# Two-chunk weight halves, a merged FFN step, and one unit's transpose on TensorE, in a kernel of block-wise linear attention followed by a bilinear FFN

## The chip, the cores and the metric

One core of one Trainium2 chip runs the whole kernel. The metric is the device time of one execution in microseconds (us), the median of the runs shown. The profile is of one execution; its span runs from the first to the last instruction.

## What is computed

The input is q, k and v (batch 4, 8 heads, 768 positions, head size 64), a decay `lam` for each head, and three weight matrices. The attention is linear with decay, computed in blocks, with a running state:

```python
intra = (q_blk @ k_blk.T * decay_mask) @ v_blk      # each batch and head
inter = (q_blk * lam_pow) @ kv_state
out_blk = intra + inter
kv_state = lam_block * kv_state + (k_blk * rev_pow).T @ v_blk
```

Its output is laid out as x, 3072 tokens by 512, and the FFN follows:

```python
a = x @ w_a          # 512 -> 1536
b = x @ w_b          # 512 -> 1536
out = (a * b) @ w_out   # 1536 -> 512
```

## The kernel before

**Units and groups.** The work is cut into 24 *units*, each one block of 128 positions of one batch element with all eight heads (six units to a batch element). Units are gathered into eight *groups* of 4, 1, 2, 4, 4, 4, 4 and 1 units (`GROUPS`). The FFN of a group runs on TensorE (PE) while the attention of later units is woven in between. The first four units are done in a packed form ahead of everything; the change does not touch them.

**One unit's attention** is made of pieces, named by letters in a hand-written plan:

- P (or PK and PV apart): the scaling of k and q to a tile `qk` in bf16, mostly on POOL (L262, L267), and the cast of v to `vb` (L276), on DVE for unit 7 and later. Then `pump()` issues further loads.
- T: `qk` transposed on PE as eight 128x128 transposes into a PSUM bank (L299), which ACT copies to `qkT` (L301). Units listed in `DMA_T` have no T: P issues a DMA transpose from SP's queue instead (L285).
- S: the scores of the unit (L313, two PSUM banks) and two masks on DVE (L330).
- V: the unit's k and v products added to a bank `kvd` (L369), and the state copied from it by DVE to `st` (L401). The next V writes the same bank.
- O, O2 and Q: the output of one unit, of two, or of two units together with the scores of the next two: products with the state (`inter`, L345), with the masked scores (L355), and the copy to the FFN's input `xT` on ACT (L362).

**The FFN of a group** has 12 *parts*, one for each 128 columns of w_a and w_b. A part is four matmuls for a and four for b (L439), a copy `a_sb` of a on ACT (L447), and a product `ab` on DVE (L452). Then come the matmuls with w_out (L472). After every part, and at points between the w_out matmuls, `hook(slot)` runs what `PLAN` lists for that group and slot: slots 0 to 11 are the parts, 12 and later lie in the w_out stage. Engines run in program order, so the plan fixes the order on every engine.

**The weights** are loaded in f32 through twelve staging buffers `wst` in the order of `pending`, and cast to bf16 by `cast_w`. w_a and w_b come in six chunks of 256 columns, which a DMA reads in rows of 1,024 bytes; w_out comes in six chunks of two row blocks, in rows of 2,048 bytes. Group 0's FFN follows the arrival: it takes the chunks in steps (`W_STEPS`), all a parts of a step before its b parts, and casts the next step's chunks meanwhile, a on DVE and b on ACT.

**Loads of q, k and v** are issued by SP in the order of `pending`. `pump()` lets them through up to a distance from the unit last prepared: `LOOKAHEAD` is 3 units at first and 2 once more than 8 units are in use, with 2 at nine units and 1 at ten. These loads, the DMA transposes and nearly all stores share SP's queue, which works in order. PSUM banks are taken in a ring of seven.

Of the kernel before, what the change touches and what calls it, by code (L numbers as in the profile page):

```python
# [22 lines left out]
def _bc(ap, dims):  # L23
# [3 lines left out]

GROUPS = (4, 1, 2, 4, 4, 4, 4, 1)
W_CHUNKS = (256,) * 6
W_STEPS = ((0, 1), (2,), (3,), (4,), (5,))  # L30
W_BUFS = 12
LOOKAHEAD = {9: 2, 10: 1}
DMA_T = (7,) + tuple(range(9, 24))
KEEP_GROUPS = 3
PACK = 4

# [8 lines left out]
        (35, "PK", 5), (35, "PV", 5)],  # L45
    1: [(0, "V", 4), (2, "T", 5), (3, "PK", 6), (6, "PV", 6), (6, "S", 5), (7, "T", 6),
        (10, "S", 6), (12, "O2", (5, 6)), (13, "P", 7)],
    2: [(0, "V", 6), (1, "P", 8), (4, "T", 8), (4, "P", 9), (8, "S", 7),
        (8, "S", 8), (9, "V", 7), (6, "P", 10), (10, "V", 8),
        (12, "Q", (7, 8, 9, 10)), (12, "P", 11), (13, "V", 9), (14, "P", 12),  # L50
        (14, "O2", (9, 10))],
    3: [(3, "S", 11), (3, "S", 12)],
# [13 lines left out]
def kernel(  # L66
# [11 lines left out]
    nc = tc.nc  # L78
    B, H, S, D = q.shape
# [46 lines left out]
    def load_x(w, u):  # L126
        b, nb = divmod(u, NB)
        t = ld_pool.tile([128, H, D], F32, name=w + "f", tag=w + "f")
        nc.sync.dma_start(out=t, in_={"q": qr, "k": kr, "v": vr}[w][b, nb])
        raw[u, w] = t  # L130

    wa_sb = singles.tile([128, KS, d_ff], BF16, name="wa_sb")
    wb_sb = singles.tile([128, KS, d_ff], BF16, name="wb_sb")
# [4 lines left out]
    staged = {}  # L138
    w_off = [sum(W_CHUNKS[:i]) for i in range(len(W_CHUNKS) + 1)]

    def load_w(kind, c):
        t = wst_pool.tile([128, 1024], F32, name="wst", tag="wst")
        if kind == "o":
            t = t[:].rearrange("p (k n) -> p k n", k=2)
            nc.sync.dma_start(out=t, in_=wo_r[:, 2 * c:2 * c + 2, :])
        else:
            w = W_CHUNKS[c]
            t = t[:, :KS * w].rearrange("p (k n) -> p k n", k=KS)
            r = wa_r if kind == "a" else wb_r
            nc.sync.dma_start(out=t, in_=r[:, :, w_off[c]:w_off[c + 1]])  # L150
        staged[kind, c] = t

    def cast_w(kind, c, eng):
        t = staged.pop((kind, c))
        if kind == "o":
            dst = wo_sb[:, 2 * c:2 * c + 2, :]
        else:
            dst = (wa_sb if kind == "a" else wb_sb)[:, :, w_off[c]:w_off[c + 1]]
        if eng == "act":
            nc.scalar.copy(dst, t)  # L160
        elif eng == "pool":
            nc.gpsimd.tensor_copy(dst[:, :, :128], t[:, :, :128])  # L162
            nc.gpsimd.tensor_copy(dst[:, :, 128:], t[:, :, 128:])
        else:
            nc.vector.tensor_copy(dst, t)
        pump()

    pending = []
    for cs in W_STEPS:
        pending += [("a", c) for c in cs] + [("b", c) for c in cs]  # L170
# [5 lines left out]
    used = {"u": 0}  # L176

    def pump():
        while pending:
            kind, c = pending[0]  # L180
            if kind in "abo":
                if len(staged) >= W_BUFS:
                    return
            elif c >= used["u"] + LOOKAHEAD.get(used["u"], 2 if used["u"] > 8 else 3):
                return
            pending.pop(0)
            if kind in "abo":
                load_w(kind, c)
            else:
                load_x(kind, c)  # L190
# [15 lines left out]
    for w, src in (("q", q), ("k", k)):  # L206
        x4_r = src[0, :, 0:PACK * BLK, :].rearrange("h (p r) d -> p h (r d)", r=PACK)
        n_h = 4 if w == "q" else 2
        for h in range(0, H, n_h):
            t = wst_pool.tile([128, 1024], F32, name=w + "4", tag="wst")[:, :n_h * 256]  # L210
            nc.sync.dma_start(out=t.rearrange("p (h x) -> p h x", h=n_h), in_=x4_r[:, h:h + n_h])
            t = t.rearrange("p (h r d) -> p h r d", h=n_h, r=PACK)
# [3 lines left out]
    for u in range(n0):  # L216
        load_x("v", u)
    pump()


# [39 lines left out]
    def make_ks(u, eng):  # L260
        qk = prep_pool.tile([128, 2, H, D], BF16, name="qk", tag="qk")
        eng_of(eng).tensor_mul(qk[:, 1], raw.pop((u, "k")),  # L262
                               lp_k[:, u % NB].to_broadcast([128, H, D]))
        U[u] = dict(qk=qk, kn=qk[:, 1])

    def make_qs(u, eng):
        eng_of(eng).tensor_mul(U[u]["qk"][:, 0], raw.pop((u, "q")),  # L267
                               lp_q[:, u % NB].to_broadcast([128, H, D]))
# [10 lines left out]
    def prep_k(u):  # L279
        make_ks(u, "dve" if u < n0 + 2 else "pool")  # L280
        make_qs(u, "pool")
        used["u"] = u + 1
        if u in DMA_T:
            qkT = qkT_pool.tile([128, 2, HP, 128], BF16, name="qkT", tag="qkT")
            nc.sync.dma_start_transpose(  # L285
                out=qkT[:].rearrange("p j hp i -> p (j hp) i"),
                in_=U[u]["qk"][:].rearrange("p j h d -> p (j h d)"))
            U[u]["qT"], U[u]["kT"] = qkT[:, 0], qkT[:, 1]
# [155 lines left out]
    def a_part(f, xT, gt, cuts=None):  # L444
        ps = half(wa_sb, f, xT, gt, "a_ps", cuts)
        a_sb = a_pool.tile([128, 512], BF16, name="a_sb", tag="a")
        nc.scalar.copy(a_sb[:, :gt], ps[:, :gt])  # L447
        return a_sb

    def b_part(f, xT, gt, a_sb, ab):  # L450
        ps = half(wb_sb, f, xT, gt, "b_ps")
        nc.vector.tensor_mul(ab[:, f, :gt], a_sb[:, :gt], ps[:, :gt])  # L452
# [22 lines left out]
    def ffn(u0, n, xT, hook, first, last):  # L475
        gt = n * BLK
        ab = ab_pool.tile([128, FC, 512], BF16, name="ab", tag="ab")
        if first:
            for i, cs in enumerate(W_STEPS):
                nxt = W_STEPS[i + 1][0] if i + 1 < len(W_STEPS) else None  # L480
                fs = range(w_off[cs[0]] // 128, w_off[cs[-1] + 1] // 128)
                a_sbs = [a_part(f, xT, gt, ((0, gt - BLK), (gt - BLK, gt)) if f == 0 else None)
                         for f in fs]
                if i == 0:
                    cast_w("b", cs[1], "act")
                elif nxt:
                    cast_w("a", nxt, "dve")
                for n_f, (f, a_sb) in enumerate(zip(fs, a_sbs)):
                    b_part(f, xT, gt, a_sb, ab)
                    hook(f)  # L490
                    if i == 0 and n_f == 1:
                        cast_w("a", nxt, "dve")
                if nxt:
                    cast_w("b", nxt, "act")
            ops = [ps_bank("op", [128, d_model], F32, hold=True) for _ in range(n)]
            slot = FC
            for c in range(FC // 2):
                for t in range(n):
                    out_mms(ops[t], ab, t, range(2 * c, 2 * c + 2))
                    if c == FC // 2 - 1:  # L500
                        store(u0 + t, ops[t], 0, d_model)
                    hook(slot)
                    slot += 1
            bank["held"].clear()
            return
        for f in range(FC):
            a_sb = a_part(f, xT, gt)
            b_part(f, xT, gt, a_sb, ab)
            hook(f)
        for t in range(n):  # L510
            op = ps_bank("op", [128, d_model], F32, ffn=True)
            if last and t == n - 1:
                for lo, hi in ((0, 256), (256, 384), (384, 512)):
                    if lo:
                        op = ps_bank("op", [128, d_model], F32, ffn=True)
                    out_mms(op, ab, t, range(FC), lo, hi)
                    store(u0 + t, op, lo, hi, nc.scalar if hi == d_model else None)
                return
            out_mms(op, ab, t, range(FC // 2))
            hook(FC + 2 * t)  # L520
            out_mms(op, ab, t, range(FC // 2, FC))
            store(u0 + t, op, 0, d_model)
            hook(FC + 2 * t + 1)
# [135 lines left out]
    for g, n in enumerate(GROUPS):  # L659
# [6 lines left out]
        def hook(slot, plan=plan):  # L666
            for name, us in plan.get(slot, ()):
                if name == "C":
                    cast_w("o", us, "dve")
                elif name == "PK":  # L670
                    prep_k(us)
                elif name == "PV":
                    prep_v(us)
                elif name == "P":
                    prep_k(us)
                    prep_v(us)
                elif name == "W":
                    store_kept()
                elif name == "T":
                    piece_T(us)  # L680
                elif name == "S":
                    piece_S(us)
                elif name == "V":
                    piece_V(us)
                elif name == "O":
                    pieces_O((us,))
                elif name == "O2":
                    pieces_O(us)
                else:
                    pieces_O(us[:2], us[2:])  # L690
# [31 lines left out]
```

## Time and profile before

| | |
|---|---|
| median of 3 runs | 235.05 us (234.89 to 235.6) |
| the profiled execution | 235.05 us, span 233.3 us |
| granted clock of PE | 1.000 |
| PE busy | 225.2 us, 97% |
| DVE, ACT, POOL busy | 117.6, 89.8, 50.7 us |
| DMA transposes | 16, median 4.3 us from issue to landing |
| loads of w_a and w_b | 12 of 512 KB, 8.6 us to landing |
| loads of q, k, v after the packed units | 64 of 256 KB, 4.6 to 5.1 us to landing |

Busy time is what an engine spent in instructions. In the timelines quoted later a line has the start in us, the time in us of a run of like instructions, engine, line of the kernel, operation, output<-inputs, their shape and how many; brackets at the end give how long the engine had stood before it and which instruction released it. In a list of waits a line says who waited for whom, the total in us, how often, and the longest.

Group 0's FFN begins at 18.4 us. Its a and b parts take until 39.6 us. Group 1's FFN lies between 51.3 and 62.2 us, group 2's between 62.2 and 85.0 us.

### The profile page before, as it was taken

To read this page: it belongs to the slowest core of one execution; us is meant where nothing else is said; L and a number is where in the kernel's file an instruction comes from. 1 tells how busy PE (TensorE), PEld (TensorE's weight loads), DVE (VectorE), ACT (ScalarE), POOL (GpSimd) and SP (SyncE) were. 2 spreads that over 40 slices of the span, in tenths; PEclk is the share of its full clock that TensorE was granted. 3 is DMA by queue.
4 is the path that set the end of the run, shared out by engine and by line. 5 is a ranking of instruction groups with operands and counts; after the bars stand their busy time and mean duration, and the time that the engine had idled before them with its cause. 6 is when DMAs were issued, how large, how long until landed. Compare 5 with 4: busy or idle time off the path is not lost.

```text
span 233.3 us, 4513 instructions
## 1 busy us (share of the span) xinstructions
PE 225.2 (97%) x1771; PEld 124.4 (53%) x1771; DVE 117.6 (50%) x204; ACT 89.8 (38%) x171; POOL 50.7 (22%) x65
## 2 busy tenths in 40 slices
PE   7898999999997999999999999999999999999994
PEld 2584444459696654454544454544454544444493
DVE  0894857536469645775235674235573224332050
ACT  3586553066451333342243342333332333332261
POOL 6052000237451552433300643001200000000000
PEclk9999999999999999999999999999999999999999
DMA  4999999999896999999959997229300220000311
GB/s 154 301 276 351 348 366 299 294 219 209 183 209 137 218 165 217 224 149 229 340 203 213 229 176 122 90 85 208 71 3 0 90 93 0 1 0 9 128 45 48
DMA packets 97477, 39.10 MB, mean 168 GB/s; under 512 B 84400, under 2 KB 92976, under 8 KB 97456
## 3 DMA queue, kind: packets, MB, share of 16 engines
q1 hardware_dynamic: 97168, 38.74, 73.9%
q8 instruction: 14, 0.23, 0.4%
q10 hardware_dynamic: 288, 0.07, 0.1%
q14 instruction: 7, 0.06, 0.1%
HBM read 28.32 MB, written 6.29 MB: 148 GB/s over the span
## 4 chain that ended last, share of the span: by engine, by line
PE 90%; DVE 3%; DMA 3%; ACT 2%; issue 1%; SPq 0%; DVEq 0%
PE a_ps L439 27%; PE b_ps L439 26%; PE op L472 26%; PE o_ps L355 3%; DMA q<-in_q_dram 3%; PE kq L313 2%; PE o_ps L345 2%; DVE m L330 2%; PE kvd L369 1%; ACT scratch L565 1%; PE tps L299 1%; DVE scratch L542 1%; DVE st L401 1%; PE kq L590 1%; PE kv L369 0%
## 5 line engine op out<-in xcount | busy, mean ns | idle before, releaser
L452 DVE TENSOR_TENSOR ab<-a_sb,b_ps 128x512 bf16<-128x512 bf16 (+2 forms) x96 | 52.2, 551 | 78.9 <-PE b_ps L439 58.1
L439 PE MATMUL a_ps<-xT,wa_sb 128*128 128x512 bf16 (+3 forms) x388 | 77.0, 324 | 0.7 <-ACT scratch L575 0.7
L439 PE MATMUL b_ps<-xT,wb_sb 128*128 128x512 bf16 (+2 forms) x384 | 77.1, 326 | 0.0
L447 ACT CAST a_sb<-a_ps 128x512 bf16<-128x512 f32 (+2 forms) x96 | 45.5, 480 | 66.2 <-PE a_ps L439 65.8
L472 PE MATMUL op<-wo_sb,ab 128*128 128x512 bf16 (+2 forms) x312 | 65.6, 363 | 0.0
L439 PEld LDWEIGHTS <-wb_sb 128*128 128x128 bf16 x384 | 34.5, 98 | 28.6 <-ACT wb_sb L160 0.2
L439 PEld LDWEIGHTS <-wa_sb 128*128 128x128 bf16 x388 | 33.9, 98 | 29.0 <-POOL wa_sb L162 0.8
L472 PEld LDWEIGHTS <-ab 128*128 128x128 bf16 x312 | 28.8, 98 | 29.9
L330 DVE TENSOR_TENSOR m<-kq,lotri 128x512 bf16<-128x512 f32 x47 | 29.3, 681 | 19.0 <-PE kq L313 18.5
L262 POOL TENSOR_TENSOR qk<-kf,lp_k 128x512 bf16<-128x512 f32 x18 | 18.8, 1042 | 75.9 <-DMA kf<-in_k_dram 66.0
L267 POOL TENSOR_TENSOR qk<-qf,lp_q 128x512 bf16<-128x512 f32 x20 | 22.1, 1105 | 22.5 <-DMA qf<-in_q_dram 22.5
L467 ACT COPY o_sb<-op 128x512 f32<-128x512 f32 (+2 forms) x19 | 10.3, 540 | 34.0 <-PE op L472 34.0
L362 ACT CAST xT<-o_ps 128x512 bf16<-128x512 f32 x22 | 12.0, 588 | 18.6 <-PE o_ps L355 18.1
L401 DVE TENSOR_TENSOR st<-kvd,bdiag 128x512 bf16<-128x512 f32 x18 | 12.3, 682 | 3.7 <-PE kvd L369 2.9
L276 DVE CAST vb<-vf 128x512 bf16<-128x512 f32 x17 | 11.1, 655 | 0.1
L198 PE MATMUL idle<-idle_sb 128*128 128x128 bf16 (+1 forms) x31 | 7.3, 376 | 1.3 <-DVE idle_sb L193 1.3
L355 PE MATMUL o_ps<-m,vb 128*64 128x128 bf16 x192 | 7.8, 222 | 0.0
L301 ACT COPY qkT<-tps 128x1024 bf16<-128x1024 bf16 x4 | 4.0, 1012 | 9.4 <-PE tps L299 9.4
L276 POOL CAST vb<-vf 128x512 bf16<-128x512 f32 x7 | 4.7, 674 | 13.4 <-DMA vf<-in_v_dram 13.4
L345 PEld LDWEIGHTS <-st 128*128 128x128 bf16 x80 | 5.4, 98 | 3.3 <-DVE st L401 0.6
L313 PE MATMUL kq<-qkT 64*128 64x128 bf16 x160 | 6.6, 218 | 0.0
L355 PEld LDWEIGHTS <-vb 128*64 128x64 bf16 x192 | 5.7, 109 | 1.4
(57 smaller groups left out, 86.1 us busy)
## 6 DMA issues: line engine op xcount, KB each, us to landing
vf<-in_v_dram SPq DMA_DIRECT2D x24, 256.0 KB, 5.1
qf<-in_q_dram SPq DMA_DIRECT2D x20, 256.0 KB, 4.6
kf<-in_k_dram SPq DMA_DIRECT2D x20, 256.0 KB, 4.6
out_dram<-o_sb SPq DMA_DIRECT2D x16, 256.0 KB, 2.0
wst<-in_moe_w_a_dram SPq DMA_DIRECT2D x6, 512.0 KB, 8.6
wst<-in_moe_w_b_dram SPq DMA_DIRECT2D x6, 512.0 KB, 8.7
wst<-in_moe_w_out_dram SPq DMA_DIRECT2D x6, 512.0 KB, 8.6
out_dram<-o_kept SPq DMA_DIRECT2D x7, 256.0 KB, 2.8
```

The lines of the kernel that those rows point to most:

```text
L262: eng_of(eng).tensor_mul(qk[:, 1], raw.pop((u, "k")), lp_k[:, u % NB].to_broadcast([128, H, D]))
L267: eng_of(eng).tensor_mul(U[u]["qk"][:, 0], raw.pop((u, "q")), lp_q[:, u % NB].to_broadcast([128, H, D]))
L276: eng_of(eng).tensor_copy(vb, vf)
L313: nc.tensor.matmul(kq[i][:, hp, :], lhsT=d["kT"][p, hp, :], rhs=d["qT"][p, hp, :], start=True, stop=True, skip_group_check=True)
L330: nc.vector.tensor_mul(m, kq[i], lotri_bc)
L355: nc.tensor.matmul(d["o"][p, hp, :], lhsT=d["vb"][:, 2 * hp + i, :], rhs=d["m"](i, hp), start=(first and hp == 0), stop=True, skip_group_c ...
L362: nc.scalar.copy(xT[:, :, col:col + BLK], o_ps)
L401: nc.vector.tensor_mul(st[:].rearrange("p hp i d -> p hp (i d)"), ps[:].rearrange("p hp i d -> p hp (i d)"), bdiag_bc)
L439: nc.tensor.matmul(ps[:, lo:hi], lhsT=w_sb[:, s, f * 128:(f + 1) * 128], rhs=xT[:, s, lo:hi], start=(s == 0), stop=(s == KS - 1), skip_gro ...
L447: nc.scalar.copy(a_sb[:, :gt], ps[:, :gt])
L452: nc.vector.tensor_mul(ab[:, f, :gt], a_sb[:, :gt], ps[:, :gt])
L472: nc.tensor.matmul(op[:, lo:hi], lhsT=ab[:, f, t * 128:(t + 1) * 128], rhs=wo_sb[:, f, lo:hi], start=(f == 0), stop=(f == FC - 1))
```

## The change

- Unit 7's `qk` is transposed on PE (a T at slot 1 of group 2) and no longer by DMA. Units 9 to 23 are transposed by DMA as before.
- In group 2 the scores of units 7 and 8 move from slot 8 to slot 6, and V of unit 7 from slot 9 to slot 7. V of unit 8 stays at slot 10. P of unit 10 stays at slot 6, but its vb cast now follows the masks on DVE.
- `LOOKAHEAD` is 3 units up to nine units in use and 2 above.
- The last two chunks of w_a and of w_b (columns 1024 to 1535) are loaded as two halves of the contraction, in rows of 512 columns (2,048 bytes), and cast as such. Both halves are needed for any of these columns.
- Group 0's FFN handles these columns in one step of four parts. The loads come in the order a, a, b, b where it was a, b, a, b, and the step before casts both a halves on DVE and both b halves on ACT.
- The store of the last 128 columns of the output goes out from ACT's queue in both kernels.

```diff
 W_CHUNKS = (256,) * 6
-W_STEPS = ((0, 1), (2,), (3,), (4,), (5,))
+W_STEPS = ((0, 1), (2,), (3,), (4, 5))
+W_HALVES = (4, 5)
 W_BUFS = 12
-LOOKAHEAD = {9: 2, 10: 1}
-DMA_T = (7,) + tuple(range(9, 24))
+LOOKAHEAD = (3, 2)
+DMA_T_FROM = 9
...
-    2: [(0, "V", 6), (1, "P", 8), (4, "T", 8), (4, "P", 9), (8, "S", 7),
-        (8, "S", 8), (9, "V", 7), (6, "P", 10), (10, "V", 8),
+    2: [(0, "V", 6), (1, "T", 7), (1, "P", 8), (4, "T", 8), (4, "P", 9), (6, "S", 7),
+        (6, "S", 8), (7, "V", 7), (6, "P", 10), (10, "V", 8),
         (12, "Q", (7, 8, 9, 10)), (12, "P", 11), (13, "V", 9), (14, "P", 12),
...
+    def w_part(w, c):
+        if c in W_HALVES:
+            j = W_HALVES.index(c)
+            return w[:, 2 * j:2 * j + 2, w_off[W_HALVES[0]]:]
+        return w[:, :, w_off[c]:w_off[c + 1]]
...
             r = wa_r if kind == "a" else wb_r
-            nc.sync.dma_start(out=t, in_=r[:, :, w_off[c]:w_off[c + 1]])
+            if c in W_HALVES:
+                t = t.rearrange("p k n -> p (k n)").rearrange("p (k n) -> p k n", k=2)
+            nc.sync.dma_start(out=t, in_=w_part(r, c))
...
-            dst = (wa_sb if kind == "a" else wb_sb)[:, :, w_off[c]:w_off[c + 1]]
+            dst = w_part(wa_sb if kind == "a" else wb_sb, c)
...
-            elif c >= used["u"] + LOOKAHEAD.get(used["u"], 2 if used["u"] > 8 else 3):
+            elif c >= used["u"] + LOOKAHEAD[used["u"] > 9]:
...
-        if u in DMA_T:
+        if u >= DMA_T_FROM:
...
             for i, cs in enumerate(W_STEPS):
-                nxt = W_STEPS[i + 1][0] if i + 1 < len(W_STEPS) else None
+                nxt = W_STEPS[i + 1] if i + 1 < len(W_STEPS) else ()
...
                 if i == 0:
                     cast_w("b", cs[1], "act")
-                elif nxt:
-                    cast_w("a", nxt, "dve")
+                else:
+                    for c in nxt:
+                        cast_w("a", c, "dve")
                 for n_f, (f, a_sb) in enumerate(zip(fs, a_sbs)):
                     b_part(f, xT, gt, a_sb, ab)
                     hook(f)
                     if i == 0 and n_f == 1:
-                        cast_w("a", nxt, "dve")
-                if nxt:
-                    cast_w("b", nxt, "act")
+                        cast_w("a", nxt[0], "dve")
+                for c in nxt:
+                    cast_w("b", c, "act")
```

## The prediction

> **What bounds the kernel now.** I read the table of busy time, then PE's waits, then the timelines of PE and DVE around the longest one, then landings.
>
> ```profile
> span 233.3 us, 4513 instructions
> PE 225.2 (97%) x1771; PEld 124.4 (53%) x1771; DVE 117.6 (50%) x204; ACT 89.8 (38%) x171; POOL 50.7 (22%) x65
> ...
> PE kvd L369 <- DVE st L401: 1.5, 1, 1.5
> PE idle L198 <- DVE idle_sb L193: 1.3, 1, 1.3
> PE a_ps L439 <- ACT scratch L575: 0.7, 1, 0.7
> PE tq L554 <- DVE scratch L542: 0.6, 3, 0.2
> PE o_ps L345 <- DVE st L401: 0.4, 1, 0.4
> PE tn L574 <- ACT scratch L565: 0.2, 1, 0.2
> ```
>
> PE is busy for 97% of the span, at full clock. The four waits not named st end before 18.4 us, ahead of everything that the diff touches. From there to the last matmuls PE stands twice, both times in the FFN of group 2 and both times for a state copy on DVE: 1.5 and 0.4 us. So the change can win at most 1.9 us, plus PE work that it removes; it can lose by PE work that it adds or by new waits. No DMA is in the list: POOL waits 66 us for loads of k, yet none of that reaches PE. The longest wait, on PE and then on DVE:
>
> ```profile
> 70.80 0.62 PE L313 MATMUL kq<-qkT 64*128 64x128 bf16 x16
> ...
> 72.24 0.39 PE L369 MATMUL kvd<-vb,qk 128*128 128x128 bf16 x4
> ...
> 75.02 0.38 PE L369 MATMUL kvd<-vb,qk 128*128 128x128 bf16 x4 [1.52 <-DVE st L401]
> ...
> 69.79 1.19 DVE L276 CAST vb<-vf 128x512 bf16<-128x512 f32 x1
> 70.91 0.74 DVE L452 TENSOR_TENSOR ab<-a_sb,b_ps 128x256 bf16<-128x256 bf16 x2
> 71.57 2.47 DVE L330 TENSOR_TENSOR m<-kq,lotri 128x512 bf16<-128x512 f32 x4
> 73.96 0.40 DVE L452 TENSOR_TENSOR ab<-a_sb,b_ps 128x256 bf16<-128x256 bf16 x1
> 74.29 0.68 DVE L401 TENSOR_TENSOR st<-kvd,bdiag 128x512 bf16<-128x512 f32 x1
> ```
>
> At slot 8 PE makes the scores of units 7 and 8 (70.80); at slot 9 V7 adds unit 7 to kvd (72.24); at slot 10 V8 wants the same bank (73.50) and may write it only when DVE has copied unit 7's state. DVE has four masks ahead of that copy, which ends at 74.97. V8 therefore stands 1.52 us.
>
> **What the Trainium skill says.** "VectorE: DVE Perf Modes", section "The three transpose paths", gives a 128x128 transpose 390 ns on TensorE and 1309 ns by DMA. The trace's eight on TensorE take 0.45 us of PE's time together (45.90 to 46.35), pipelined, so I use that; the DMA form of all eight blocks lands 4.3 us after its issue (median). "DMA: Bandwidth & Descriptors", section "Queues, rings and completion order", says that each DMA engine takes its descriptors in ring order; here loads and transposes that SP issues land in the order of issue, so what SP issues first delays the rest. "SBUF — State Buffer", section "Who interferes with whom", says that some DVE copies and casts share a port pair with GpSimd and that the later one waits fully. The trace agrees: L276 on DVE takes 0.42 us alone (67.38) and 1.19 where POOL had begun just before (69.79). Masks keep 0.68 either way.
>
> **The change part by part.**
>
> *Unit 7 transposed on PE (slot 1 of group 2).* Adds eight matmuls: +0.45 us on PE, which has no idle time there. Its qk is ready at 57.6 (POOL), PE is there at 64.15: no wait. Its copy on ACT takes 1.01 us (row L301) and holds up the a_sb of the next two parts by under 1 us; unit 8's copy does this now at 67.4 with no wait of PE. SP loses the transpose of 61.73 to 63.47, so unit 10's loads, queued behind it, are issued up to 1.8 us earlier.
>
> *Scores 7 and 8 from slot 8 to 6, V7 from 9 to 7, V8 still at 10.* PE's work is equal. With the 0.45 added, the scores start at 69.40 and V8's turn is at 73.67. Unit 8's transpose (slot 4) ends at 67.8, its ACT copy at 68.9: ready. DVE: masks from 69.95 to 72.35 (4 x 0.60); then vb of unit 10, which now follows the masks: 0.35 alone, up to 1.0 if POOL holds the port (unit 11's scaling, 2.1 us, would be about there); then one ab product 0.35 and the state copy 0.65. It ends between 73.7 and 74.3. So V8 waits 0.1 to 0.6 us; I take 0.35, **1.17 less**. What is late next is the same copy, not a new thing.
>
> *The wait of 0.40 at unit 10's inter product (82.68).* DVE's masks for 9 and 10, a vb of 1.24 us (80.78, beside POOL's k scaling of unit 12) and a state copy stand before it. Unit 12's load moves earlier, so the port should be free and the vb cost 0.4: the wait goes, or stays at 0.4. I take 0.1 left, **0.30 less**.
>
> *Loads of unit 11 let through one step earlier (LOOKAHEAD).* Now SP issues the transposes of 9 and 10 first (66.11 and 70.73, landing 71.9 and 73.9) and then the loads of 11 (72.00). After, three loads of 1.2 us each go ahead of both transposes. Unit 10's load is earlier by up to 1.8 us. From v of unit 9 landing at 64.7: six loads to 71.9, then two transposes at 1.1 to 2.2 us each (the distances of 65.8 to 64.7 and of 71.9 to 69.7): unit 10's lands at 74.1 to 76.3. Scores 9 and 10 want them at about 76.6 and 76.9 (slot 12; 77.95 now, less the gain). Covered by 0.6 to 2.8 us, so nothing; without that cover 1.4 us at most if an instruction fetch of about a microsecond, as at 69.9 us, falls on each. DMA is idle from 70.0 to 71.7 now, so the later loads come sooner, if anything.
>
> *Halves in rows of 2,048 bytes.* The last a and b chunks land 1.50 us apart now, w_out's chunks, which have such rows, 1.39 apart: four loads win 0.4 us of DMA. PE doesn't wait for DMA, so nothing.
>
> *One step of four parts, a loads first.* PE needs both halves of a at 32.68 and both of b at 36.13. Landings by order of issue: 29.6, 31.1, 32.6, 34.1 at the latest. DVE's casts (0.69) end at 31.8: 0.9 us spare. ACT's casts (1.05) end at 35.2: 0.9 spare. They hold back the copy of part 8, which is then ready at 35.7, before part 8's product at 37.0. Four parts fit the seven banks and the five a_sb buffers, as in the first step. The w_out casts at hooks 8 and 9 now sit between products: 0.3 us on DVE, with w_out's matmuls of these parts far later (48 us). Nothing; up to +0.8 if a landing slips by two chunks' distance.
>
> *From 83 us on* PE has no idle time, so a gain at 75 us carries to the end. The next tight place is the scores of units 13 and 14 at 99.80, 1.5 us after unit 14's transpose lands (98.3); PE comes 1 us earlier and the loads too.
>
> **Sum:** +0.45 - 1.17 - 0.30 = -1.02 us. The profiled execution took 235.05 us (span 233.3 and 1.75 around it), which is also the median: **234.0 us**.
>
> **Rivals.**
>
> *The gain isn't there (within 0.3%).* The vb cast and POOL collide for a full operation (another 0.5), the 0.40 stays, and unit 10's transpose is 0.3 late: -1.02 + 0.25 + 0.3 + 0.3 = -0.17, so 234.9. For: two such collisions are seen in this very stage. Against: they need POOL to be busy just then.
>
> *Slower: the transposes of 9 and 10 come too late, behind unit 11's loads.* Place: scores 9 and 10 at 76.6 us. It decides once unit 10's transpose lands more than 1.7 us after its turn, at 78.6. Price: if each transpose takes the 2.2 us of unit 9's and the queue is another 2 to 3 us behind (unit 8's v landed 3.0 us after its k, with nothing of its own to explain it), landing is 78.5 to 79.5, a wait of 1.6 to 2.6; with the V8 wait at 0.6 and the 0.40 kept: +0.45 - 0.92 + 2.1 = +1.6, so 236.6. For: the kernel before lets both transposes ahead. Against: the queue has an idle stretch to absorb it.
>
> *The last weights come late for the merged step.* All four loads are needed 1.7 us closer together. A slip of 2 us would cost about 1.1: 235.1. Against: the landings are evenly spaced.
>
> That the change doesn't do what it says: the words also name a last store from ACT's queue, but the last 128 columns go there before and after; no effect.
>
> **How the numbers follow.** What a measurement of this kernel can tell from no change is about 0.3%, 0.7 us. The forecast's own range is 233.5 to 234.5, chance 0.54; the unchanged case 0.22, the late weights 0.06; slower 0.18. A part of the forecast's upper end lies over 234.35, so faster 0.50, same 0.27, slower 0.23. For 8 in 10 the range goes from 233.4 to 236.0, leaving out the worse half of the slower case and a gain above 1.65.
>
> **What would show it.** Right: PE's wait at kvd L369 falls from 1.5 to 0.6 or less; tps L299 has 40 matmuls, qkT copies on ACT are five, DMA transposes 15; no wait of PE between 18.4 and 70 us; scores 9 and 10 start at about 76.6. Wrong: a wait of kq L313 for DMA, a wait for wa_sb or wb_sb casts, or a kvd wait still over 1 us.

## The result and the profile after

The changed kernel took 233.41 us (233.08 to 233.85), the kernel before, measured beside it, 234.96 (234.7 to 235.6): a ratio of **0.9931** (0.9912 to 0.995; a ratio is estimated from the executions and can differ a little from the quotient of the medians). It is faster, by about 1.5 us. The forecast was 234.0, with a range of 233.5 to 234.5, so the gain is larger than forecast and the time lies just below the range. The profiled execution took 233.47 us with a span of 231.6.

The page's first lines after, and then the list of PE's waits (who waited for whom, total in us, how often, longest):

```profile
span 231.6 us, 4530 instructions
PE 225.1 (97%) x1779; PEld 124.8 (54%) x1779; DVE 114.1 (49%) x204; ACT 90.6 (39%) x172; POOL 50.1 (22%) x65
```

```profile
PE idle L207 <- DVE idle_sb L202: 1.3, 1, 1.3
PE tq L564 <- DVE scratch L552: 1.1, 4, 0.3
PE a_ps L448 <- POOL wa_sb L171: 0.4, 1, 0.4
PE tn L584 <- ACT scratch L575: 0.2, 1, 0.2
```

PE has eight matmuls more, and both waits for a state copy are gone from the list. What is left ends by 18.3 us. Lines are numbered nine or ten higher than before (L439 is L448, L369 is L378). PE and DVE around the place of the old wait, after:

```profile
69.42 0.62 PE L322 MATMUL kq<-qkT 64*128 64x128 bf16 x16
...
70.86 0.39 PE L378 MATMUL kvd<-vb,qk 128*128 128x128 bf16 x4
...
73.73 0.38 PE L378 MATMUL kvd<-vb,qk 128*128 128x128 bf16 x4
...
76.66 0.62 PE L322 MATMUL kq<-qkT 64*128 64x128 bf16 x16
...
69.93 2.48 DVE L339 TENSOR_TENSOR m<-kq,lotri 128x512 bf16<-128x512 f32 x4
72.33 0.41 DVE L285 CAST vb<-vf 128x512 bf16<-128x512 f32 x1
72.66 0.41 DVE L461 TENSOR_TENSOR ab<-a_sb,b_ps 128x256 bf16<-128x256 bf16 x1
72.99 0.68 DVE L410 TENSOR_TENSOR st<-kvd,bdiag 128x512 bf16<-128x512 f32 x1
```

V7 and V8 are the two `kvd` lines, at 70.86 and 73.73. The state copy ends at 73.67, and V8 starts at 73.73 with no bracket behind it: nothing is left of the wait, and nothing to spare either. Scores of 9 and 10 follow at 76.66; unit 10's DMA transpose had landed at 74.8.

Where the 1.7 us of span lie, by starts of matmuls: the FFN of group 2 runs from the first a of group 2 to the first a of group 3. Before, and then after:

```profile
62.18 0.60 PE L439 MATMUL a_ps<-xT,wa_sb 128*128 128x256 bf16 x4
...
85.00 1.03 PE L439 MATMUL a_ps<-xT,wa_sb 128*128 128x512 bf16 x4
```

```profile
62.09 0.60 PE L448 MATMUL a_ps<-xT,wa_sb 128*128 128x256 bf16 x4
...
83.14 1.03 PE L448 MATMUL a_ps<-xT,wa_sb 128*128 128x512 bf16 x4
```

That is 22.82 us before and 21.05 after: **1.77 less**. The other groups take the same to 0.01 us; the start is 0.1 earlier, and the part behind the last matmul takes 0.16 longer.

### The profile page after: what moved, and what is told of

Read it like the earlier page. It is cut to its first block, busy times and chain, and to the rows that moved or that the text cites. A ratio compares the mean times of both kernels' runs of the same rounds, so it can differ in the third digit from the quotient of the medians.

```text
span 231.6 us, 4530 instructions
## 1 busy us (share of the span) xinstructions
PE 225.1 (97%) x1779; PEld 124.8 (54%) x1779; DVE 114.1 (49%) x204; ACT 90.6 (39%) x172; POOL 50.1 (22%) x65
## 4 chain that ended last, share of the span: by engine, by line
PE 91%; SPq 4%; DMA 3%; issue 0%; POOL 0%; ACT 0%
PE a_ps L448 27%; PE op L481 27%; PE b_ps L448 27%; SPq L130 3%; DMA wst<-in_moe_w_a_dram 3%; PE o_ps L364 3%; PE kq L322 2%; PE o_ps L354 2%; SPq L220 1%; PE kvd L378 1%; PE tps L308 1%; PE kvd L399 0%; POOL wa_sb L171 0%; ACT o_sb L476 0%
## 5 line engine op out<-in xcount | busy, mean ns | idle before, releaser
L448 PE MATMUL a_ps<-xT,wa_sb 128*128 128x512 bf16 (+3 forms) x388 | 76.9, 324 | 0.4 <-POOL wa_sb L171 0.4
L448 PE MATMUL b_ps<-xT,wb_sb 128*128 128x512 bf16 (+2 forms) x384 | 76.9, 326 | 0.0
L481 PE MATMUL op<-wo_sb,ab 128*128 128x512 bf16 (+2 forms) x312 | 65.6, 363 | 0.0
L448 PEld LDWEIGHTS <-wb_sb 128*128 128x128 bf16 x384 | 34.5, 98 | 28.6 <-ACT wb_sb L169 0.2
L448 PEld LDWEIGHTS <-wa_sb 128*128 128x128 bf16 x388 | 33.9, 98 | 28.7 <-POOL wa_sb L171 0.6
L271 POOL TENSOR_TENSOR qk<-kf,lp_k 128x512 bf16<-128x512 f32 x18 | 19.7, 1094 | 75.4 <-DMA kf<-in_k_dram 62.4
L276 POOL TENSOR_TENSOR qk<-qf,lp_q 128x512 bf16<-128x512 f32 x20 | 21.0, 1051 | 22.3 <-DMA qf<-in_q_dram 22.3
L310 ACT COPY qkT<-tps 128x1024 bf16<-128x1024 bf16 x5 | 5.1, 1012 | 11.6 <-PE tps L308 11.6
L285 DVE CAST vb<-vf 128x512 bf16<-128x512 f32 x17 | 8.2, 482 | 0.0
```

Of the source, the lines that this page charges most:

```text
L271: eng_of(eng).tensor_mul(qk[:, 1], raw.pop((u, "k")), lp_k[:, u % NB].to_broadcast([128, H, D]))
L285: eng_of(eng).tensor_copy(vb, vf)
L448: nc.tensor.matmul(ps[:, lo:hi], lhsT=w_sb[:, s, f * 128:(f + 1) * 128], rhs=xT[:, s, lo:hi], start=(s == 0), stop=(s == KS - 1), skip_gro ...
L481: nc.tensor.matmul(op[:, lo:hi], lhsT=ab[:, f, t * 128:(t + 1) * 128], rhs=wo_sb[:, f, lo:hi], start=(f == 0), stop=(f == FC - 1))
```

## The experiments

Twelve runs, two of them of the two kernels unchanged and one a repetition. Ratios are to the kernel before, measured beside each on the same chip; times in us from different chips should not be compared. "Stage" is the time of group 2's FFN by starts, as above, in the profiled execution.

| kernel | ratio (95%) | stage, us | PE's waits in it, us listed |
|---|---|---|---|
| before, first profile | | 22.82 | 1.52 and 0.40 |
| before, again | 0.9982 (0.9961 to 1.0004) | 22.14 | 1.40 |
| weights alone | 0.9994 (0.9982 to 1.0007) | 22.01 | 1.28 |
| LOOKAHEAD alone | 0.9993 (0.9976 to 1.001) | 22.39 | 1.52 |
| T7 on PE alone | 0.9981 (0.9969 to 0.9992) | 22.52 | 1.28 |
| T7 on PE and slots | 0.9937 (0.9917 to 0.9956) | 21.21 | none |
| slots alone | 0.9923 (0.9904 to 0.9942) | 20.60 | none |
| slots alone, again | 0.991 (0.9892 to 0.9928) | 20.60 | none |
| changed, T7 back to DMA | 0.9924 (0.9904 to 0.9944) | 20.60 | none |
| changed, first profile | 0.9931 (0.9912 to 0.995) | 21.05 | none |
| changed, again | 0.9936 (0.9917 to 0.9955) | 21.74 | 0.42 |
| changed, vb first | 0.9918 (0.9889 to 0.9947) | 21.05 | none |
| changed, V8 early | 0.9965 (0.9944 to 0.9985) | 21.92 | 0.74 |
| slots, T8 by DMA too | 0.9932 (0.9907 to 0.9957) | 21.34 | 0.93 |

### One part at a time

**Weights alone**: `W_HALVES`, the merged `W_STEPS` and their loads and casts; the rest as before.

> The kernel before with the weight halves and the merged step of four parts alone. Theory W (the gain is the removal of the two waits for state copies in group 2, each worth the shift in PE's start times and not the idle time listed): no change, 235.0 us within 0.3; both waits stand (about 1.5 and 0.4 us listed), PE has no wait between 18.4 and 70 us. Rival L (the part of the gain over the two listed waits, some 0.3 us, comes from the lighter weight loads): 234.6.

234.36 us, ratio 0.9994: no change, within 0.2%. Only the kvd wait stands in the stage, at 1.28. The loads did get lighter (SP's queue carried 96,144 packets, 97,168 before), but PE stood for none of these chunks before or after. Rival L falls. The first wait is shorter here than the 1.52 of the first profile:

```profile
74.81 0.38 PE L378 MATMUL kvd<-vb,qk 128*128 128x128 bf16 x4 [1.28 <-DVE st L410]
```

DVE's cast of unit 10's v, ahead of the masks, took 0.42 us here (at 69.60) and 1.19 in the first profile of before, where POOL had begun. In the profiles with 0.42 (this and T7 on PE alone) the wait is 1.28, in those with 1.19 to 1.28 it is 1.40 to 1.52. So up to 0.24 us of the first wait goes with that collision.

**LOOKAHEAD alone.**

```diff
-LOOKAHEAD = {9: 2, 10: 1}
+LOOKAHEAD = (3, 2)
```

> The kernel before with the new LOOKAHEAD alone. Theory W: the wait of 1.5 us at kvd stays; the vb cast of unit 11 on DVE (1.24 us beside POOL before) takes 0.4 because unit 12's load comes earlier, so the second wait, 0.4 us listed and 0.57 by start times, goes: 234.4 us. Rival Q (the transposes of 9 and 10 come late behind unit 11's loads, with unit 7's transpose still in the queue): unit 10's lands after 77.9, a wait of 0.5 to 1.5 us at kq, 235.0 to 236.0 us.

234.43 us, ratio 0.9993: neither the expected 0.57 nor Rival Q's loss. Unit 10's transpose landed at 76.7, 2.8 us later than before, and its scores at 77.8 still found it. The kvd wait kept 1.52, the second was absent, as the theory had it; but "Before, again" below shows the old LOOKAHEAD without it too.

**T7 on PE and slots**: the four entries of `PLAN[2]` and unit 7 out of `DMA_T`, the rest as before.

> The kernel before with unit 7's transpose on PE and the moved slots, with the old LOOKAHEAD and the old weight loads. Theory W: the first wait goes (1.68 us by start times), 0.45 us of transposes is added, the second wait stays at 0.4 listed: 235.0 - 1.68 + 0.45 = 233.8 us. Rival L: 0.3 less is gained, 234.1 us.

233.04 us, ratio 0.9937: the whole of the change's gain without the weights and without LOOKAHEAD. It is 1.5 us below the kernel before beside it, where the theory had 1.2, and the second wait, which was to stay, is not listed.

**Slots alone**: S 7 and S 8 at slot 6, V 7 at slot 7, unit 7 by DMA.

```diff
-(8, "S", 7), (8, "S", 8), (9, "V", 7), (6, "P", 10), (10, "V", 8),
+(6, "S", 7), (6, "S", 8), (7, "V", 7), (6, "P", 10), (10, "V", 8),
```

> The kernel before with the scores of 7 and 8 at slot 6 and V of 7 at slot 7, nothing else; unit 7 still by DMA. Theory W: its transpose lands at 65.8 us and the scores ask at 69.0, so no wait for it; the first wait goes without the 0.45 us of PE's transposes, the second stays: 233.3 to 233.5 us. Rival D (the slots need unit 7 on PE because its DMA transpose is too late): a wait at kq, 234 us or more.

232.81 us, ratio **0.9923**; Rival D falls. Unit 7's DMA transpose lands at 65.1, and the scores start at 68.99 without waiting:

```profile
68.99 0.62 PE L313 MATMUL kq<-qkT 64*128 64x128 bf16 x16
...
73.29 0.38 PE L369 MATMUL kvd<-vb,qk 128*128 128x128 bf16 x4
```

Its stage is 0.45 us shorter than that of the changed kernel: the eight transposes, and nothing else.

**T7 on PE alone**, with the slots of before:

> The kernel before with unit 7 transposed on PE at slot 1 and its slots left as they were. Theory W: eight transposes add 0.45 us to PE; the wait at kvd keeps 1.3 to 1.5 us listed, since scores, masks and both V's all move by the same 0.45; ratio 1.002. Rival D (taking the transpose out of SP's queue is itself worth something): 1.000 or less.

234.56 us, ratio 0.9981, where 1.002 was expected. The wait stayed, as predicted, and the stage is 0.51 longer than with the weights alone, where the wait had the same 1.28 and the second was absent as well: the transposes are paid. Yet the median is not worse. The lowest time is not better than that of before (234.15 and 234.01); it is the long executions that are missing (highest 235.24 and 235.91). This interval is against the expectation, and one trace doesn't settle it: that the shorter SP queue makes collisions of DVE and POOL rarer fits, but wasn't isolated.

### Is the second wait part of the kernel before?

**Before, again**, unchanged:

> The kernel before, unchanged, profiled once more. Theory J: its second wait (0.40 us listed, unit 10's inter product) is not part of the kernel but of one execution, in which DVE's cast of v and POOL's scaling of unit 12 fell together; here it is absent or of another size, with a span of 232.6 to 233.0 us without it and the first wait still at 1.3 to 1.5. Rival C: it is caused by the old LOOKAHEAD and stands again at 0.3 to 0.5, span about 233.3.

Theory J holds for this execution: the span is 232.6, and the wait of 0.40 is absent. Two executions of this kernel are traced; how often the others have the wait is not known. DVE in the two executions of the same kernel, first profile and then second, each beside POOL's scaling:

```profile
80.78 1.24 DVE L276 CAST vb<-vf 128x512 bf16<-128x512 f32 x1
81.94 0.68 DVE L401 TENSOR_TENSOR st<-kvd,bdiag 128x512 bf16<-128x512 f32 x1
...
80.70 1.04 POOL L262 TENSOR_TENSOR qk<-kf,lp_k 128x512 bf16<-128x512 f32 x1 [1.73 <-PE op L472]
```

```profile
80.59 0.42 DVE L276 CAST vb<-vf 128x512 bf16<-128x512 f32 x1
80.92 0.68 DVE L401 TENSOR_TENSOR st<-kvd,bdiag 128x512 bf16<-128x512 f32 x1
...
80.73 1.18 POOL L262 TENSOR_TENSOR qk<-kf,lp_k 128x512 bf16<-128x512 f32 x1 [1.79 <-PE kvd L369]
```

In the first POOL starts 0.08 us ahead of DVE, and the cast takes 1.24; in the second DVE is 0.14 ahead, takes 0.42, and POOL is the one drawn out. So 0.2 us in the start of two instructions decide on 0.8 us of DVE. The late cast ends 0.28 us after POOL's operation (82.02 and 81.74): it waits for the whole of what POOL has left. The second wait was listed in none of the other kernels of the table.

**Changed, again**, unchanged:

> The changed kernel, unchanged, beside the three others on one chip: 0.993 to 0.995 of before. By start times the change is worth 1.1 us where the kernel before has only its first wait (0.9953) and 1.7 to 1.8 where it has the second as well (0.9925).

0.9936. Here the same collision struck the cast of unit 10, ahead of the state copy. DVE, POOL and PE:

```profile
72.13 0.98 DVE L285 CAST vb<-vf 128x512 bf16<-128x512 f32 x1
...
73.36 0.68 DVE L410 TENSOR_TENSOR st<-kvd,bdiag 128x512 bf16<-128x512 f32 x1
...
71.78 1.04 POOL L276 TENSOR_TENSOR qk<-qf,lp_q 128x512 bf16<-128x512 f32 x1
...
74.09 0.38 PE L378 MATMUL kvd<-vb,qk 128*128 128x128 bf16 x4 [0.42 <-DVE st L410]
```

POOL holds the port from 71.78, the cast takes 0.98 in place of 0.41, and V8 stands 0.42. In the first profile POOL's two operations were over by 71.84:

```profile
69.80 1.04 POOL L271 TENSOR_TENSOR qk<-kf,lp_k 128x512 bf16<-128x512 f32 x1 [1.64 <-DMA kf<-in_k_dram]
70.80 1.04 POOL L276 TENSOR_TENSOR qk<-qf,lp_q 128x512 bf16<-128x512 f32 x1
```

So the stage of the changed kernel was seen with two lengths, 21.05 and 21.74, and that of the kernel before too, 22.14 and 22.82. LOOKAHEAD has a part in this risk. These POOL operations scale unit 11, and with the new LOOKAHEAD they begin at 69.8 to 73.3 in every profile; with the old one they begin at 75.4 or later, well behind this cast. That is read from the traces, not tested.

**Changed, vb first**: P of unit 10 ahead of the scores at slot 6.

> The changed kernel with P of unit 10 listed ahead of the scores at slot 6, so that the vb cast runs on DVE before the four masks, as it did in the kernel before. DVE's work is equal and only its order differs. Theory P (shared port): the cast now falls beside POOL's scaling of unit 11 (69.8 us); if POOL has begun, the cast takes 1.2 us in place of 0.4, everything behind it is 0.8 later, and V8 starts at about 74.5 in place of 73.73: 234.2 us. Rival N (the order on DVE doesn't matter): 233.4 us, no wait.

233.22 us, ratio 0.9918. The cast ran at 70.06 in 0.42 us, ahead of POOL's operation at 70.74, and no wait came. The collision that Theory P needed didn't happen, so this decides neither way; it shows only that equal DVE work in another order ends at the same place (stage 21.05).

### What is a wait worth?

**Changed, V8 early**: V of unit 8 at slot 9.

> The changed kernel with V of unit 8 at slot 9 in place of 10: the wait is put back by 0.87 us of PE work less between the two V's. The state copy ends at 73.67 as before. Theory S: V8 starts at 73.7 again, so the start of the w_out matmuls moves by the whole 0.87 us, while the list of waits shows only about 0.70, because the idle time is counted from the modelled end of the last matmul, 0.16 us after the next one could have started. Time 234.2 to 234.3 us. Rival T: the shift equals the listed idle time, or PE makes it up later; 234.1 or less.

234.19 us, ratio 0.9965, and the list of PE's waits shows 0.7. The timeline:

```profile
70.69 0.39 PE L378 MATMUL kvd<-vb,qk 128*128 128x128 bf16 x4
73.56 0.38 PE L378 MATMUL kvd<-vb,qk 128*128 128x128 bf16 x4 [0.74 <-DVE st L410]
...
76.82 0.39 PE L354 MATMUL o_ps<-qkT,st 128*128 128x128 bf16 x4
```

From V7 to V8 it is 2.87 us, exactly as in the changed kernel (70.86 to 73.73), though one part less stands between them. The stage grew by 0.87 us, 21.05 to 21.92, the whole part that had been moved behind the wait. The idle time listed, 0.74, is 0.13 less than that. Theory S holds.

### Can it be better still?

**Slots, T8 by DMA too**: unit 8 in `DMA_T`, its scores at slot 8.

> The kernel before with unit 8 transposed by DMA as well (no T in group 2), scores of 7 at slot 6, V of 7 at slot 7, scores of 8 at slot 8; the old LOOKAHEAD. Theory W: PE loses another 0.45 us of transposes against the kernel with the moved slots alone (0.9923 of before), and V8 needs only the masks of unit 7 ahead: 0.9923 - 0.0019 = 0.990. Rival Q: two more transposes in SP's queue make unit 8's scores, wanted at about 70.3 us, or those of unit 10, wanted at 75.8, wait for DMA: 0.993 or more.

0.9932, where Theory W had 0.990: Rival Q's wait came. The interval overlaps that of the slots alone (0.9904 to 0.9942), so the times don't tell which is better; in the profiles this stage is 0.74 us longer. The transposes of 7 and 8 landed at 65.6 and 71.7, and PE stood for the second:

```profile
71.78 0.40 PE L313 MATMUL kq<-qkT 64*128 64x128 bf16 x8 [0.93 <-DMA qkT<-qk]
```

Its 22 executions spread from 232.31 to 235.76, and the lowest is below every one of the slots alone (232.68 to 233.09, on other chips, where the lowest times of before were within 0.14 us of those here). So this version may win where the transpose lands in time; no trace shows such an execution.

**Slots alone, again**, beside the changed kernel:

> The kernel before with the three moved slots alone, a second time, beside the changed kernel: 0.45 us less than that (0.0019 in the ratio) by PE's work, so 0.991 to 0.993. Rival: no difference to the changed kernel, as DMA transposes cost as much elsewhere.

**Changed, T7 back to DMA**:

> The changed kernel with unit 7's transpose given back to DMA. Theory W: 0.45 us less than the changed kernel, equal to the kernel before with moved slots: 0.991 to 0.993. Rival Q: with the new LOOKAHEAD three loads and one transpose stand ahead of the transposes of 9 and 10; unit 10's scores, wanted at 76.4 us, wait for DMA by up to 0.5 us, and nothing is gained on the changed kernel.

232.97 us (0.991) and 233.14 (0.9924), the changed kernel 233.45 (0.9936) on the same chip. The intervals overlap, but the stage is 0.45 us shorter in each of the three profiles without the PE transposes. In the second of these kernels group 3 took 0.39 us longer, with a wait of 0.2 at the scores of units 13 and 14 for a DMA transpose: Rival Q's mechanism, a group later than expected. On each of the two chips where it ran, the kernel before with its three moved slots had the lowest median, 232.81 and 232.97 us.

## Why the prediction was right or wrong

**In short.** Direction, place and mechanism of the main gain were right. The step that failed is the size of the waits in the sum: "V8 waits 0.1 to 0.6 us; I take 0.35, 1.17 less", and beside it "I take 0.1 left, 0.30 less" for the second wait. By starts, the first profiles show 1.69 us gone at V8 and 0.57 at the second place. The medians differ by 1.55 us, where 1.02 was forecast.

**Right: the bound and the place.** PE's own work set the end, and only group 2's two waits could move. Weights, merged step and the wider LOOKAHEAD were put at nothing, and alone each measured within 0.1% of before, and no interval reaches 0.3% away.

**Right: the times of the working.** Scores of 7 and 8 at 69.40 (measured 69.42), masks from 69.95 (69.93), the copy's end at 73.7 to 74.3 (73.67, and 74.04 in the second profile), scores of 9 and 10 at about 76.6 (76.66), unit 10's transpose landing at 74.1 to 76.3 (74.8), T7 at 0.45 us of PE (0.45).

**Too small: "1.17 less".** Two errors are in it. What was left was taken as a middle value, where the runs show two cases: nothing, or 0.42 listed when POOL has the port. And what was removed was taken as the 1.52 listed. By starts it is more: V7 is followed by one part and V8, so V8 would have started at 72.24 + 0.22 + 0.87 = 73.33; it started at 75.02, **1.69** later.

**Too small and not sure: "the wait of 0.40 at unit 10's inter product", "0.30 less".**

```profile
81.89 0.39 PE L345 MATMUL o_ps<-qkT,st 128*128 128x128 bf16 x4
82.68 0.40 PE L345 MATMUL o_ps<-qkT,st 128*128 128x128 bf16 x4 [0.40 <-DVE st L401]
```

By starts it cost 0.57 (81.89 + 0.22 = 82.11 to 82.68), not 0.40. What the prediction expected of the cast did happen: unit 12's k landed at 77.27 in place of 80.54, POOL had done with unit 12 at 79.46, and the cast at 79.49 took 0.41. But the kernel before, unchanged, ran without this wait in its second profile, as did the kernels with the old LOOKAHEAD. That the change ends it for good is therefore not shown; what failed is to count a wait seen in one execution as a fixed part of the kernel.

**The sum again**, for the two first profiles: +0.45 - 1.69 - 0.57 = -1.81, measured -1.77 in the stage. The forecast of -1.02 was short by 0.35 and 0.10 for waits assumed to remain, and by 0.17 for each of the two prices read from the list.

**How much of it is chance.** Where unit 10's cast took its 0.42 and the second wait was absent, the stage was 22.01 with the slots of before (weights alone) and 21.05 with those of the change, 0.96 apart. The other 0.81 between the first profiles are the effect of two collisions, at 69.8 and 80.8 us, that the first profile of before had and the first of the changed kernel had not. That the forecast lies near 0.96 is luck, since its two gains include a part of both collisions. The medians, 1.5 to 1.7 us apart, lie between the two figures, which fits collisions in many executions of the kernel before. The spread fits as well: on one chip the slots alone took 232.68 to 232.93 us in six executions, and the kernel before 234.12 to 235.59 in 27. But only one execution of each run is traced.

**The slower rival**, transposes of 9 and 10 too late, did not decide: unit 10's landed 1.9 us ahead of the first use. Its mechanism is real, since it struck unit 8 in one experiment (0.93 us) and group 3 in another (0.39).

**Left open.** Why T7 on PE alone measured 0.2% faster than before, how often each collision occurs, and why the part behind the last matmul varies between 3.06 and 3.55 us over these profiles.

## What to carry to other kernels

When a wait of a pipelined engine goes, price it by the starts of its instructions (when it started, less when it would have), not by the idle time listed; here that was 0.17 us more for each of the two waits. Before a wait enters a sum, look for it in a second execution: one that hangs on which of two engines takes a shared port first is an event with a chance, and belongs in the range. And where a change bundles several edits, the order of a few entries can be the whole of it: here three moved slots did all the gain, and the transpose that came with them gave back 0.45 us.

## What the runs showed of the hardware

- A DVE cast of 128x512 from f32 takes 0.42 us alone. Where it was held up by a POOL scaling that had begun before it, it ended 0.28 to 0.29 us after that operation, so it took 1.24 where POOL had begun 0.08 us earlier and 0.98 where it had begun 0.35 us earlier. Started 0.14 us ahead of POOL it keeps 0.42, and POOL's takes 1.18 in place of 1.04. That one side waits is in the Trainium skill ("SBUF — State Buffer", "Who interferes with whom"), and these traces agree; that the same kernel falls on either side from one execution to the next, with 0.7 us of a 22 us stage, was not expected.
- Eight 128x128 transposes on PE shift what follows by 0.45 us. The same work by DMA cost PE nothing where it landed in time: at 65.1 us for a use at 69.0 (slots alone). A second one, behind three loads in the queue, landed at 71.7 for a use at 70.9.
